# Attention scores on four 64x64 quadrants of TensorE instead of two 64x128 halves, with 192 keys a tile instead of 256

## The chip, the cores and the metric

The kernel runs on one core of one Trainium2 chip. A core has a matrix engine (TensorE, PE in the profile; its weight loads are shown as PEld), a vector engine (VectorE, DVE), a scalar engine (ScalarE, ACT), GpSimd (POOL) and SyncE (SP), which issues the DMAs here. PE reads SBUF and writes PSUM, which has eight banks of 512 fp32 values on each of 128 partitions. The metric is the device time of one execution in microseconds (us), lower is better; the time before is the median of three runs.

## The reference

Eight batches of eight heads, 576 positions, head size 64. Attention is causal in a window of 128 keys, with a linear bias by distance; its result goes through a gated feed-forward layer. Cut to what matters:

```python
scores = scale * np.matmul(q, k.transpose(0, 1, 3, 2))
rel = pos[:, None] - pos[None, :]
bias = slopes[:, None, None] * (-np.abs(rel))[None]
mask = (rel >= 0) & (rel < 128)
scores = np.where(mask, scores + bias[None], -1e9)
attn = softmax(scores)                     # max subtracted
x = np.matmul(attn, v)                     # heads side by side: 4608 tokens x 512
out = (sigmoid(x @ w_gate) * (x @ w_val)) @ w_out      # 512 -> 1536 -> 512
```

Each query sees exactly 128 keys (fewer at the start of a sequence): its own and the 127 before it.

## The kernel before

**Units and blocks.** Two heads of a batch make a unit, 32 units in all. The two sequences of a unit stand one behind the other, 1152 positions, cut in nine blocks of 128 queries. A block needs the keys of its own block and of the block before; block 0 has only its own.

**Scores** (`scores`, L373 to L417). Blocks are taken in groups, of four for the first 72 blocks (18 groups) and of eight after that (27 groups). Head size 64 is the contraction, so a score matmul uses only half the rows of PE: the queries of alternate blocks are laid in partitions 0 to 63 and in 64 to 127 (`by_parity` on the host; keys are stored twice, once in each half), so that two blocks run in the two row halves. For each block one fp32 matmul (L390) has the 128 queries as its stationary operand and 256 keys (block 0: 128) moving. It writes 128 partitions (queries) by 256 columns (keys of the block before, then of its own) of PSUM. A bank holds two such tiles; the banks `mm2` to `mm5` (`sp`) serve the scores, the row halves in different ones. PE records each fp32 matmul as two passes, each with its own weight load.

**Folding.** Of the 256 columns a query needs 128. A predicated copy on DVE (L403) takes, for each pair of tiles in a bank, every column of the own block that lies in the query's future and puts the score of the same column of the block before in its place; `before` is the mask, an upper triangle of ones. Then DVE adds the bias and finds the extreme of each row (L411, biases in `relm`), ACT takes the exponential (L414).

**Probabilities and values.** For three blocks at a time: reciprocal of the sums (DVE, L429, L431), the scaling (ACT L434 or DVE L435), a transpose on PE (L439) into bank `mm6`, a copy to SBUF (`both`, ACT), and two selections on POOL (L450) that spread each column to own and previous keys. For each unit 13 matmuls (L476) multiply with the values; they have 64 stationary columns, so the two heads use the two column halves of PE.

**Feed-forward.** A third of its first projection (L528, banks `mm0` and `mm1`) over the first 3072 tokens is mixed in between the attention steps, once four units of a batch are done. The rest (L662) and the output projection (L780) use a block form with seven products for eight and come after the attention. Their weights are unpacked and split in two parts by ACT and DVE (`prepare`, `prepare2`).

**What sets the order.** Every step is added to a `Graph` with its engine, an estimated cost, what it reads and writes and a wish `want`. `Graph.order` plays a list schedule: of all steps that are ready it takes the one that could start first, and steps of ACT may be moved to DVE or from DVE to POOL. All engines' instructions are then emitted by planned start. A cost thus moves instructions on every engine. While PE has little to do at the very start, `warm` matmuls (L252) fill it.

**At the start** DVE builds the masks and biases (L219 to L236) before the planned steps begin.

The names that the steps below use: L390 score matmul, L403 fold, L411 bias and extreme, L439 transpose, L476 values, L528 first projection.

Of the kernel before, what the change touches and what calls it, by code (L numbers as in the profile page):

```python
# [9 lines left out]
I32 = mybir.dt.int32  # L10
F32R = mybir.dt.float32r
AF = mybir.ActivationFunctionType
ALU = mybir.AluOpType
PSUM = bass.MemoryType.PSUM

P = 128
B, H, S, D = 8, 8, 576, 64
# [137 lines left out]
def dve_cost(n, psum=False, two=False):  # L155
    return 0.07 + n * (0.00104 if psum or two else 0.00053)
# [7 lines left out]
def attention_gated_ffn(ctx: ExitStack, tc: tile.TileContext, qd, kd, vd, wg, wv, wo, out):  # L164
    nc = tc.nc
# [39 lines left out]
    rel = moe.tile([P, 3, P], F32, tag="pi0", name="rel")  # L205
# [4 lines left out]
    def keep(tag, *shape):  # L210
        n, (t, a) = 1, spare.get(tag) or (moe.tile([P, (2 if tag[0] == "h" else KC) * 2 * N2], F32, tag=tag, name=f"early_{tag}"), 0)
        for x in shape:
            n *= x
        spare[tag] = t, a + n
        names = " ".join("abc"[:len(shape)])
        return t[:, a:a + n].rearrange(f"p ({names}) -> p {names}", **dict(zip("abc", shape)))

    before = keep("h3", 2, P).bitcast(I32)
    nc.vector.tensor_scalar(rel[:, 1], rel[:, 0], 0.0, None, op0=ALU.is_lt)  # L219
    for a in range(2):  # L220
        nc.vector.tensor_copy(before[:, a], rel[:, 1])
    nc.vector.scalar_tensor_tensor(rel[:, 2], rel[:, 1], float(P), rel[:, 0], op0=ALU.mult, op1=ALU.add)
    relm = [keep("h3" if p < 2 else "h4", 5, P) for p in range(NPAIR)]
    f = -8.0 * 2.0 ** -1
# [19 lines left out]

    mm = [ps_m.tile([P, NB], F32, name=f"mm{i}") for i in range(8)]
    sp = [t.rearrange("p (a q) -> p a q", a=2) for t in mm[2:6]]
    tp, avp = mm[6].rearrange("p (a q) -> p a q", a=4), mm[7]
    TP, TAIL, AVP = ("mm", 6), ("mm", 6, TRI), ("mm", 7)

# [99 lines left out]
    def slot(x, u, shape):  # L349
        return slots[x] if u.l == NSLOT - 1 and x in slots else T(att, f"{x}{u.l}", [P, *shape], F32)  # L350

    kraw = lambda u: slot("kr", u, [TOK])
    qraw = lambda u: slot("qr", u, [(NBLK + 1) // 2, P])
# [15 lines left out]
    def three_of(u, i):  # L369
        m = u.n * TRI + i // TRI  # L370
        e = i % TRI
        st = lambda: T(att, f"st{m % NST}", [P, 9], F32)
        pb = lambda: T(att, f"pb{m % NPB}", [P, TRI, P], F32) if m % NPB > 1 else kept[m % NPB]  # L373
        return m, e, st, pb, ("st", m % NST), ("pb", m % NPB)

    def scores(blks):

        u0, i0 = blks[0]
        want = u0.when(i0)
        slack = 0.0 if u0.n < HEAD else SLACK  # L380
        spot = [(k % 2, k // 2) for k in range(len(blks))]
        half = len(blks) == RUN // 2 and stages[0] % 2
        stages[0] += 1
        bank_of = lambda r, a: r * (RUN // 4) + a // 2 + half

        def matmuls():
            for (u, i), (r, a) in zip(blks, spot):
                lo = P if i == 0 else 0
                rows = slice(r * D, r * D + D)
                nc.tensor.matmul(sp[bank_of(r, a)][:, a % 2, lo:], qraw(u)[rows, i // 2],  # L390
                                 kraw(u)[rows, (i - 1) * P + lo:(i + 1) * P], start=True, stop=True)

        used = {}
        for (u, i), (r, a) in zip(blks, spot):
            used.setdefault(bank_of(r, a), []).append((u, i, a % 2))
        cost = sum(max(0.216 if i == 0 else 0.432 for (u, i), (r, b) in zip(blks, spot) if b == a) for a in {a for r, a in spot})
        g.add("PE", cost, matmuls, [("qr", u.l, i) for u, i in blks] + [("kr", u.l, j) for u, i in blks for j in (i - 1, i) if j >= 0],
              [("mm", 2 + b) for b in used], want, slack=slack, release=max(u.rel(i) for u, i in blks), mode=1)
        for b, on in sorted(used.items(), key=lambda kv: blks.index(kv[1][0][:2])):
            a = [a for u, i, a in on if i]  # L400
            if a:
                a0, a1 = a[0], a[-1] + 1
                g.add("DVE", dve_cost((a1 - a0) * P, psum=True), lambda b=b, a0=a0, a1=a1: nc.vector.copy_predicated(  # L403
                    sp[b][:, a0:a1, P:], before[:, a0:a1], sp[b][:, a0:a1, 0:P]), ["before"], [("mm", 2 + b)], want)
        for (u, i), (r, a) in zip(blks, spot):
            def one(u, i, b, a):
                m, e, st, pb, kst, kpb = three_of(u, i)
                want = u.when(i)
                mid = NBLK // 2
                w = 0 if i == 0 else 1 if i < mid else min(4, i - mid + 2)  # L410
                g.add("DVE", 0.21, lambda: nc.vector.tensor_tensor_reduce(  # L411
                    pb()[:, e], sp[b][:, a, P:], relm[u.p][:, w], op0=ALU.add, op1=ALU.min,
                    scale=-0.125, scalar=3.0e38, accum_out=st()[:, e:e + 1]), [("mm", 2 + b)], [(kpb, e), (kst, e)], want)
                g.add("ACT", 0.39, lambda: nc.scalar.activation(  # L414
                    pb()[:, e], pb()[:, e], AF.Exp, bias=st()[:, e:e + 1], scale=-1.0, accum_out=st()[:, 3 + e:4 + e]),
                    [(kst, e)], [(kpb, e), (kst, 3 + e)], want)
            one(u, i, bank_of(r, a), a % 2)  # L417
            if i % TRI == TRI - 1:
                probabilities(u, i - TRI + 1)
            if i == NBLK - 1:  # L420
                values(u)

    def probabilities(u, i0):
        m, _, st, pb, kst, kpb = three_of(u, i0)
        want = u.when(i0 + TRI)
        slack = 0.0 if u.n < HEAD else SLACK
        n, kb = TRI, ("both", m % NBOTH)
        both = lambda: T(att, f"both{m % NBOTH}", [P, TRI, P], F32)
        g.add("DVE", 0.07, lambda: nc.vector.tensor_scalar_add(st()[:, 6:9], st()[:, 3:6], 1.0e-9),  # L429
              [(kst, 3 + e) for e in range(n)], [(kst, 6)], want)  # L430
        g.add("DVE", 0.09, lambda: nc.vector.reciprocal(st()[:, 6:9], st()[:, 6:9]), [], [(kst, 6)], want)  # L431
        for e in range(n):
            args = lambda e=e: (pb()[:, e], pb()[:, e], st()[:, 6 + e:7 + e])
            g.add("ACT", 0.3, lambda args=args: nc.scalar.mul(*args()), [(kst, 6)], [(kpb, e)], want,  # L434
                  ways=[("DVE", 0.16, True, lambda args=args: nc.vector.tensor_scalar_mul(*args()))])  # L435

        def transpose():
            for e in range(n):
                nc.tensor.transpose(tp[:, e], pb()[:, e], ident)  # L439

        g.add("PE", 0.11 * n + 0.1, transpose, [(kpb, e) for e in range(n)], [TP], want, slack=slack)
        copy(lambda: both(), lambda: tp[:, 0:n], n * P, [TP], [kb], want, psum=True)
        for own in range(2):
            step, cmp, mult = ([1, P], ALU.is_ge, -1) if own else ([-1, P], ALU.is_gt, 1)

            def spread(own=own, step=step, cmp=cmp, mult=mult):
                f0 = 2 * i0 + own
                nc.gpsimd.affine_select(pt(u)[:, f0:f0 + 2 * n - 1:2, :], both(), [[0, n], step], cmp, 0.0,  # L450
                                        base=0, channel_multiplier=mult)

            g.add("POOL", 0.13 + 0.12 * n, spread, [kb], [("pt", u.n % NPT, i0 + e, own) for e in range(n)], want)
# [361 lines left out]
    for u in units:  # L815
        if u.n + NSLOT - 1 < len(units):
            load(units[u.n + NSLOT - 1])
        while at < (u.n + 1) * NBLK:
            n = RUN // 2 if at < SOON * NBLK else RUN
            scores(stream[at:at + n])  # L820
            at += n
        if u.n == 0:
            todo = [(src, kind, i) for i0 in range(0, FC1, GRP) for src, kind in ((wg, "g"), (wv, "v")) for i in range(i0, i0 + GRP)]
            for k, (src, kind, i) in enumerate(todo):
                prepare(w1, src, kind, i, W0 + WSTEP * k)
        if u.p == NPAIR - 1:
            while todo1 and (todo1[0] + 1) * NB <= (u.b + 1) * S:
                if todo1[0] >= LATE and banks[0] == 2:
                    banks[0] = 8
                    g.add("PY", 0.0, lambda: None, [], [TP, TAIL], FIRST)  # L830
                ffn(todo1.pop(0), w1)
# [54 lines left out]
    for e in range(4):  # L886
        m, p = 6 + e // 2, e % 2
# [60 lines left out]
```

## Time and profile before

| | |
|---|---|
| median of three runs | 1014.79 us (1013.95 to 1015.31) |
| the profiled execution, its own time | 1015.13 us |
| its span, first to last instruction | 1013.4 us |
| granted TensorE clock | 0.999 |
| PE, PEld, DVE, ACT, POOL busy | 997.5, 927.8, 784.1, 544.6, 125.1 us |
| score matmuls L390, first to last start | 5.1 to 285.8 us |
| values matmuls L476, first to last start | 19.3 to 307.9 us |

Busy time of PE is not PE at its peak: a matmul's record reaches to the end of its pipeline, so records overlap. A row of the grouped view reads: line, engine, operation, tiles written and read, shape, count; then the busy time in us, the mean of one in ns; then the idle time of the engine just before and who ended it. A row of the timeline reads: start in us, length in us, engine, line, operation, tiles, shape of most, count. A row of the chain reads: start, length, what.

### The profile page before, as it was taken

The page shows a single profiled execution, that of the slowest core. Times are in us where ns is not written, and L with a number is a line of the kernel's source. Part 1 is how long each engine was busy: PE and PEld are TensorE (multiplying, and loading weights), DVE is VectorE, ACT ScalarE, POOL GpSimd, SP SyncE. Part 2 cuts the span into 40 slices and gives each one's busy share as a digit, 9 for nine tenths or more (in the row PEclk, how much of TensorE's full clock was granted, in tenths as well). Part 3 has the DMA queues.
Part 4 walks back from the last instruction along what each step waited for, and adds up shares of the span by engine and source line. Part 5 has one row for each costly group of instructions (what it writes and reads, how often), then busy time and mean ns, then how long its engine had stood idle before and what let it go on. Part 6 is the DMA issues. An engine that isn't in the chain of part 4 may idle for free.

```text
span 1013.4 us, 18087 instructions
## 1 busy us (share of the span) xinstructions
PE 997.5 (98%) x6216; PEld 927.8 (92%) x6216; DVE 784.1 (77%) x2025; ACT 544.6 (54%) x1435; POOL 125.1 (12%) x218
## 2 busy tenths in 40 slices
PE   9899899999999999999999999999999999999998
PEld 7677678777888999999999999999999999999998
DVE  7999799967856997964976768848478877869783
ACT  6899879768753545533553535435354443434341
POOL 2343344323330000000000000000000000000000
PEclk9999999999999999999999999999999999999999
DMA  8777677847434452411553453536886354543501
GB/s 287 252 253 260 218 243 233 289 153 230 156 123 157 146 177 85 141 63 63 200 190 120 144 184 121 197 138 219 325 332 196 102 168 139 161 149 102 179 24 63
DMA packets 84284, 176.82 MB, mean 174 GB/s; under 512 B 7648, under 2 KB 50016, under 8 KB 84192
## 3 DMA queue, kind: packets, MB, share of 16 engines
q1 hardware_dynamic: 84192, 175.67, 51.2%
q8 instruction: 49, 0.80, 0.3%
q14 instruction: 43, 0.35, 0.1%
HBM read 117.44 MB, written 58.20 MB: 173 GB/s over the span
## 4 chain that ended last, share of the span: by engine, by line
PE 83%; DVE 8%; ACT 5%; DMA 2%; issue 1%; SPq 0%; ACTq 0%; DVEq 0%
PE mm L662 38%; PE mm L780 26%; PE mm L528 8%; PE mm L476 4%; PE mm L390 4%; PE mm L439 2%; ACT pb L414 2%; ACT both L185 1%; DVE first L194 1%; ACT pb L434 1%; DVE mm L403 1%; DMA wraw<-in_moe_w_gate_dram 1%; DVE w2s L194 1%; DVE pb L411 1%; DMA early_xr<-xs 1%
## 5 line engine op out<-in xcount | busy, mean ns | idle before, releaser
L662 PE MATMUL mm<-xc,w2s 128*128 128x384 f32 x2352 | 410.2, 335 | 1.0 <-ACT low L185 0.9
L662 PEld LDWEIGHTS mm<-xc,w2s 128*128 128x128 f32 x2352 | 407.4, 188 | 3.8 <-ACT low L185 2.2
L780 PE MATMUL mm<-duo,wo 128*128 128x384 f32 x1512 | 262.2, 334 | 0.0
L780 PEld LDWEIGHTS mm<-duo,wo 128*128 128x128 f32 x1512 | 262.1, 188 | 0.0
L528 PE MATMUL mm<-first,first 128*128 128x512 f32 x564 | 148.6, 403 | 0.7 <-DVE early_hs L547 0.4
L450 POOL TENSOR_SCALAR_AFFINE_SELECT pt<-both 128x384 f32<-128x384 f32 x192 | 106.6, 579 | 191.7 <-ACT both L185 178.3
L528 PEld LDWEIGHTS mm<-first,first 128*128 128x128 f32 x564 | 100.6, 188 | 21.3 <-issue 1.3
L673 ACT ACTIVATE sg<-mm 128x384 f32<-128x384 f32 x112 | 54.9, 492 | 115.9 <-PE mm L662 63.6
L669 DVE TENSOR_TENSOR mm<-mm,low 128x384 f32<-128x384 f32 x112 | 63.0, 564 | 70.0 <-PE mm L662 66.4
L185 ACT COPY low<-mm 128x384 f32<-128x384 f32 x110 | 53.0, 481 | 75.9 <-PE mm L662 64.6
L414 ACT ACTIVATE pb<-pb,st 128x128 f32<-128x128 f32 x216 | 85.0, 400 | 8.9 <-DVE st L411 8.8
L476 PEld LDWEIGHTS mm<-pt,vr 128*64 128x64 f32 x832 | 61.2, 137 | 12.7 <-issue 7.6
L194 DVE TENSOR_TENSOR duo<-rows,duo 128x768 fp32r<-128x768 f32 x66 | 62.9, 957 | 10.6 <-ACT duo L185 8.6
L185 ACT CAST duo<-rows 128x768 fp32r<-128x768 f32 x48 | 40.0, 837 | 54.1 <-PE mm L780 29.5
L476 PE MATMUL mm<-pt,vr 128*64 128x256 f32 (+2 forms) x832 | 67.4, 306 | 0.6 <-POOL pt L450 0.6
L185 ACT COPY both<-mm 128x384 f32<-128x384 f32 x96 | 46.0, 479 | 34.6 <-PE mm L439 23.5
L403 DVE COPY_PREDICATED mm<-early_h,mm 128x256 f32<-128x256 int32 (+1 forms) x144 | 49.2, 392 | 9.8 <-PE mm L390 9.3
L390 PE MATMUL mm<-kr,qr 64*128 64x256 f32 (+1 forms) x396 | 55.1, 381 | 0.2 <-DMA kr<-in_k_dram 0.2
L411 DVE CUSTOM_DVE_ANT_0 pb<-mm,early_h 128x128 f32<-128x128 f32 x216 | 51.7, 282 | 0.0
L390 PEld LDWEIGHTS mm<-kr,qr 64*128 64x128 f32 x396 | 38.1, 186 | 9.4 <-issue 2.3
L439 PE MATMUL mm<-ident,pb 128*128 128x128 f32 x216 | 38.1, 284 | 7.1 <-ACT both L185 5.9
L439 PEld LDWEIGHTS mm<-ident,pb 128*128 128x128 f32 x216 | 24.7, 140 | 21.3 <-ACT both L185 9.8
(117 smaller groups left out, 1128.0 us busy)
## 6 DMA issues: line engine op xcount, KB each, us to landing
hid<-later_hs SPq DMA_DIRECT2D x56, 384.0 KB, 2.3
rows<-hid SPq DMA_DIRECT2D x48, 384.0 KB, 3.9
kr<-in_k_dram SPq DMA_DIRECT2D x21, 576.0 KB, 4.4
wo<-stash_o SPq DMA_DIRECT2D x12, 896.0 KB, 7.7
vr<-in_v_dram SPq DMA_DIRECT2D x32, 288.0 KB, 3.2
xs<-xt SPq DMA_DIRECT2D x32, 288.0 KB, 2.8
stash_o<-wtmp SPq DMA_DIRECT2D x12, 768.0 KB, 3.4
rows_xr<-hid SPq DMA_DIRECT2D x24, 384.0 KB, 3.4
```

The costliest lines, as they stand in the source:

```text
L185: g.add("ACT", act_cost(n, psum), lambda: nc.scalar.copy(out(), src()), reads, writes, want, release=release, ways=[("DVE", dve_cost(n, ps ...
L194: g.add("DVE", dve_cost(n, psum, True), lambda: nc.vector.tensor_tensor(out(), a(), b(), op=ALU.subtract), reads, writes, want, port=not p ...
L390: nc.tensor.matmul(sp[bank_of(r, a)][:, a % 2, lo:], qraw(u)[rows, i // 2], kraw(u)[rows, (i - 1) * P + lo:(i + 1) * P], start=True, stop= ...
L411: g.add("DVE", 0.21, lambda: nc.vector.tensor_tensor_reduce(pb()[:, e], sp[b][:, a, P:], relm[u.p][:, w], op0=ALU.add, op1=ALU.min, scale= ...
L414: g.add("ACT", 0.39, lambda: nc.scalar.activation(pb()[:, e], pb()[:, e], AF.Exp, bias=st()[:, e:e + 1], scale=-1.0, accum_out=st()[:, 3 + ...
L439: nc.tensor.transpose(tp[:, e], pb()[:, e], ident)
L450: nc.gpsimd.affine_select(pt(u)[:, f0:f0 + 2 * n - 1:2, :], both(), [[0, n], step], cmp, 0.0, base=0, channel_multiplier=mult)
L476: nc.tensor.matmul(to()[e * D:(e + 1) * D, a - e * S - t0:b - e * S - t0], vraw(u)[:, c], seen, start=first, stop=last, skip_group_check=True)
L528: nc.tensor.matmul(mm[s][:, 0:wd], w.tile(kind, wi, i)[:, c * P:(c + 1) * P], xpart(x, c)[:, 0:wd], start=(k == 0 and c == 0), stop=(k == ...
L662: nc.tensor.matmul(mm[b][:, 0:N2], w.tile2(i, wp)[:, wk, c * P:(c + 1) * P], combo(k, xp)[:, c], start=(start and c == 0 and j == 0), stop ...
L669: g.add("DVE", dve_cost(N2, psum=True), lambda: nc.vector.tensor_tensor(o(), bk(b)(), a(), op=ALU.add), [("mm", b), *reads] if okeys else ...
L780: nc.tensor.matmul(mm[b][:, 0:N2], wo2(2 * q + m, wp)[:, k, j * P:(j + 1) * P], duo(xp)[:, m], start=(k in (0, 3, 1) and q == 0 and m == 0 ...
```

## The change

Each block of 128 queries becomes two tiles of 64 queries. The stationary operand has 64 rows (head size) and 64 columns (queries), so a tile uses one quadrant of PE: the row half is that of the block as before, and the first 64 queries write PSUM partitions 0 to 63, the last 64 write 64 to 127. A 64-query tile needs three runs of 64 keys, 192 instead of 256. A block's PSUM tile keeps its 256 columns, seen as four slots of 64, and slots 1 and 2 are where the folded scores end:

- first 64 queries: slots 1, 2, 3 get the keys in reversed order of runs, own first half, previous second half, previous first half; slot 0 is not written by a matmul
- last 64 queries: slots 0, 1, 2 get previous second half, own first half, own second half; slot 3 is not written

One predicated copy per pair of tiles, as before, takes slot 3 into slot 1 and slot 0 into slot 2 where the mask says so; the mask is now zero for the first 64 queries in slot 2. The slots that no matmul writes are set to zero once at the start, since the copy reads them. Block 0 of a sequence writes slots 1 and 2 only. The planner's cost of a pair of full blocks goes from 0.432 to 0.33; nothing else of it is changed.

```diff
-    before = keep("h3", 2, P).bitcast(I32)
+    before = keep("h3", 4, D).bitcast(I32).rearrange("p (a s) q -> p a s q", a=2)
     nc.vector.tensor_scalar(rel[:, 1], rel[:, 0], 0.0, None, op0=ALU.is_lt)
     for a in range(2):
-        nc.vector.tensor_copy(before[:, a], rel[:, 1])
+        nc.vector.tensor_copy(before[:, a], rel[:, 1].rearrange("p (s q) -> p s q", q=D))
+        nc.vector.memset(before[0:D, a, 1], 0)
...
     sp = [t.rearrange("p (a q) -> p a q", a=2) for t in mm[2:6]]
+    for t in sp:
+        nc.vector.memset(t.rearrange("p a (s q) -> p a s q", q=D)[:, :, 0::3], 0.0)
...
+        quads = lambda b: sp[b].rearrange("p a (s q) -> p a s q", q=D)
         def matmuls():
+            todo = [[] for _ in range((len(blks) + 1) // 2)]
+            order = [a for a in range(len(todo)) for h in range(2)]
             for (u, i), (r, a) in zip(blks, spot):
-                lo = P if i == 0 else 0
-                rows = slice(r * D, r * D + D)
-                nc.tensor.matmul(sp[bank_of(r, a)][:, a % 2, lo:], qraw(u)[rows, i // 2],
-                                 kraw(u)[rows, (i - 1) * P + lo:(i + 1) * P], start=True, stop=True)
+                todo[a].append((u, i, r, a))
+            for h in (0, 1) * len(todo):
+                for u, i, r, a in todo[order.pop(0)]:
+                    rows = slice(r * D, r * D + D)
+                    keys = kraw(u)[rows].rearrange("p (t q) -> p t q", q=D)
+                    to = quads(bank_of(r, a))[h * D:(h + 1) * D, a % 2]
+                    if i == 0:
+                        to, keys = to[:, 1:3], keys[:, 0:2]
+                    elif h == 0:
+                        last = 2 * i - 3
+                        to, keys = to[:, 1:4], keys[:, 2 * i:(last if last >= 0 else None):-1]
+                    else:
+                        to, keys = to[:, 0:3], keys[:, 2 * i - 1:2 * i + 2]
+                    nc.tensor.matmul(to, qraw(u)[rows, i // 2, h * D:(h + 1) * D], keys, start=True, stop=True)
...
-        cost = sum(max(0.216 if i == 0 else 0.432 for (u, i), (r, b) in zip(blks, spot) if b == a) for a in {a for r, a in spot})
+        cost = sum(max(0.216 if i == 0 else 0.33 for (u, i), (r, b) in zip(blks, spot) if b == a) for a in {a for r, a in spot})
...
-                    sp[b][:, a0:a1, P:], before[:, a0:a1], sp[b][:, a0:a1, 0:P]), ["before"], [("mm", 2 + b)], want)
+                    quads(b)[:, a0:a1, 1:3], before[:, a0:a1], quads(b)[:, a0:a1, 3::-3]), ["before"], [("mm", 2 + b)], want)
...
-                    pb()[:, e], sp[b][:, a, P:], relm[u.p][:, w], op0=ALU.add, op1=ALU.min,
+                    pb()[:, e], sp[b][:, a, D:D + P], relm[u.p][:, w], op0=ALU.add, op1=ALU.min,
```

On PE, a group of eight blocks in the middle of the attention reads before as follows (`mm2` to `mm5` are the score banks, `kr1` and `early_h2` keys, `qr1` and `early_xr` queries; the shape is partitions by columns written):

```order
L390 MATMUL mm2_148<-kr1_172,qr1_174 128x256
L390 MATMUL mm4_150<-early_h2_154,early_xr_155 128x128
L390 MATMUL mm2_148<-early_h2_154,early_xr_155 128x256
L390 MATMUL mm4_150<-early_h2_154,early_xr_155 128x256
L390 MATMUL mm3_149<-early_h2_154,early_xr_155 128x256
L390 MATMUL mm5_151<-early_h2_154,early_xr_155 128x256
```

The two rows that follow repeat the last two. Now such a group (another one, near the same place) ends as follows; the eight rows ahead of these are the same with `mm2` and `mm4`, and the score line is now L408:

```order
L408 MATMUL mm3_151<-kr1_178,qr1_180 64x192
L408 MATMUL mm5_153<-kr1_178,qr1_180 64x192
L408 MATMUL mm3_151<-kr1_178,qr1_180 64x192
L408 MATMUL mm5_153<-kr1_178,qr1_180 64x192
L408 MATMUL mm3_151<-early_h2_160,early_xr_161 64x128
L408 MATMUL mm5_153<-early_h2_160,early_xr_161 64x192
L408 MATMUL mm3_151<-early_h2_160,early_xr_161 64x128
L408 MATMUL mm5_153<-early_h2_160,early_xr_161 64x192
```

Eight matmuls became sixteen; of a pair of blocks the two first halves stand ahead of the two second halves, row halves alternating.

On DVE, the end of the preparation and the first folds read before (`early_h3` holds masks and the first biases, `early_h4` biases):

```order
L236 TENSOR_SCALAR early_h3_78<-early_h3_78 128x640
L236 TENSOR_SCALAR early_h4_83<-early_h3_78 128x640 x2
L403 COPY_PREDICATED mm2_148<-early_h3_78,mm2_148 128x128
L403 COPY_PREDICATED mm4_150<-early_h3_78,mm4_150 128x2x128
L411 ISA early_h2_154,st0_194<-mm2_148,early_h3_78 128x128
```

and now:

```order
L237 TENSOR_SCALAR early_h3_78<-early_h3_78 128x640
L237 TENSOR_SCALAR early_h4_85<-early_h3_78 128x640 x2
L249 MEMSET mm2_150 128x2x2x64
L249 MEMSET mm3_151 128x2x2x64
L249 MEMSET mm4_152 128x2x2x64
L249 MEMSET mm5_153 128x2x2x64
L420 COPY_PREDICATED mm2_150<-early_h3_78,mm2_150 128x128
L420 COPY_PREDICATED mm4_152<-early_h3_78,mm4_152 128x2x128
```

Four writes to PSUM have come between the biases and the first fold; the folds themselves keep their place and shape.

## The prediction

> **What bounds the kernel now.** I read the page first, for the span and the share of each engine, then the windows, to see where the engines are full, then the chain of work that ended last.
>
> ```profile
> span 1013.4 us, 18087 instructions
> PE 997.5 (98%) x6216; PEld 927.8 (92%) x6216; DVE 784.1 (77%) x2025; ACT 544.6 (54%) x1435; POOL 125.1 (12%) x218
> PE 83%; DVE 8%; ACT 5%; DMA 2%; issue 1%; SPq 0%; ACTq 0%; DVEq 0%
> ```
>
> TensorE holds 83% of the chain. The change lies in the attention stage alone, so the mean over the span is not enough. The windows (columns: PE, weight loads, DVE, ACT, POOL, each busy time and count) cut that stage in three:
>
> ```profile
> 20.00:130.00 110.00, 100.66 (x797) 77.14 (x794) 98.32 (x469) 98.97 (x381) 41.62 (x72) 1.00 0.73 247
> 130.00:180.00 50.00, 49.59 (x368) 39.42 (x366) 45.67 (x195) 44.73 (x161) 24.06 (x38) 1.00 0.75 237
> 180.00:290.00 110.00, 109.90 (x804) 87.94 (x806) 86.62 (x461) 81.20 (x315) 33.99 (x67) 1.00 0.61 201
> ```
>
> Up to 130 us PE leaves 9.3 of 110 us idle, and DVE and ACT leave 11.7 and 11.0: three engines, closely coupled. From 130 on PE has no idle time, while DVE and ACT still have a tenth to a quarter. The chain says the same. At 85 us it runs over ACT; from 186 us it runs over PE, score matmuls (L390) included. At 85 us:
>
> ```profile
> 85.41 0.58 ACT pb L414 x3
> 85.98 0.58 ACT xt L185 x2
> 86.56 0.28 ACT both L185
> 86.83 0.75 ACT pb L414 x3
> ```
>
> and from 186 us:
>
> ```profile
> 193.69 0.33 PE mm L439 x3
> 194.02 1.93 PE mm L390 x15
> 195.95 2.01 PE mm L476 x24
> 197.96 0.48 PE mm L439 x3
> 198.43 1.63 PE mm L528 x7
> ```
>
> So a shorter score step is worth its full length from about 182 us, little before 130 us.
>
> **The change, part by part.** *One score group.* The timeline has a group of eight blocks (16 records, since each matmul is recorded as two passes, each with its own weight load) and a group of four. The four:
>
> ```profile
> 25.82 1.13 PE L390 MATMUL mm<-kr,qr 64*128 64x256 f32 x8
> ```
>
> and the eight:
>
> ```profile
> 105.03 1.99 PE L390 MATMUL mm<-kr,qr 64*128 64x256 f32 x16
> ```
>
> Four blocks more cost 0.86 us. They are four passes more on each half of the rows (two blocks of two passes), and the halves run side by side, so a pass of 256 keys takes 0.86/4 = 0.215 us, and 1.99 - 8 x 0.215 = 0.27 us is fixed. With 192 keys a pass takes 0.215 x 192/256 = 0.161 us, if four quadrants run as fully side by side as two halves do now. The fixed part holds one weight load that nothing covers. Its size goes by columns:
>
> ```profile
> L390 PEld LDWEIGHTS mm<-kr,qr 64*128 64x128 f32 x396 | 38.1, 186 | 9.4 <-issue 2.3 <-DVE st L431 1.1 <-DVE st L411 0.9
> L476 PEld LDWEIGHTS mm<-pt,vr 128*64 128x64 f32 x832 | 61.2, 137 | 12.7 <-issue 7.6 <-POOL pt L450 4.0
> ```
>
> 64 columns instead of 128 save 186 - 137 = 49 ns. A group of eight then takes 8 x 0.161 + 0.22 = 1.51 us, 0.48 less; a group of four saves 4 x 0.054 + 0.05 = 0.265. The first block of a sequence has 128 keys before and after; it stands in one half only, and the other half's chain of full blocks sets the length, so it changes nothing.
>
> *Do four run at once?* No row shows 64 x 64 tiles. Two row halves run at once (L390), and two column halves over all rows do (L476). What matters is whether a tile waits for matmuls ahead of it in the program that belong to another tile. Its program order in each set of values matmuls is:
>
> ```order
> L476 MATMUL mm_153<-pt_469,vr_184 64x256
> L476 MATMUL mm_153<-pt_469,vr_184 64x192
> L476 MATMUL mm_153<-pt_469,vr_184 64x256 x4
> L476 MATMUL mm_153<-pt_469,vr_184 64x128
> L476 MATMUL mm_153<-pt_469,vr_184 64x192
> ```
>
> The last two are head 0 (first columns, 128 wide) and then head 1 (other columns, 192 wide). Two stretches of 10 ns of one such set, 40 ns apart, grouped by form, show what is in flight. The first, at 108.74 us:
>
> ```profile
> L476 PE MATMUL mm<-pt,vr 128*64 128x256 f32 x2 | 0.5, 379 | 0.0
> L476 PE MATMUL mm<-pt,vr 128*64 128x192 f32 x1 | 0.3, 326 | 0.0
> ```
>
> and the second, at 108.78 us:
>
> ```profile
> L476 PE MATMUL mm<-pt,vr 128*64 128x256 f32 x2 | 0.5, 379 | 0.0
> L476 PE MATMUL mm<-pt,vr 128*64 128x192 f32 x1 | 0.3, 326 | 0.0
> L476 PE MATMUL mm<-pt,vr 128*64 128x128 f32 x1 | 0.3, 272 | 0.0
> ```
>
> The 192-wide one has started while the 128-wide one, which stands ahead of it, has not; that one joins only later. So a column tile overtakes both passes of the other tile's matmul. [...]
>
> The weight loads have to keep up too. At the end of a set, matmuls of 64 columns follow each other:
>
> ```profile
> L476 PE MATMUL mm<-pt,vr 128*64 128x64 f32 x8 | 0.4, 221 | 0.0
> ```
>
> Eight are in flight in one 10 ns stretch, 221 ns each: one starts every 28 ns, and each has its own load of 64 columns. Four quadrants need four in 161 ns, and 4 x 28 = 112. I therefore take 0.161.
>
> *Where the groups stand.* Counts of the line's records in 131 to 182 us:
>
> ```profile
> L390 PE MATMUL mm<-kr,qr x70: 269/376/480, 131.9 to 175.5; 64*128 64x256 f32 x64, 64*128 64x128 f32 x6
> L390 PE MATMUL mm<-early_h,early_xr x26: 269/376/480, 147.9 to 176.3; 64*128 64x256 f32 x22, 64*128 64x128 f32 x4
> ```
>
> and in 182 to 300 us:
>
> ```profile
> L390 PE MATMUL mm<-kr,qr x144: 269/376/480, 187.7 to 285.8; 64*128 64x256 f32 x128, 64*128 64x128 f32 x16
> L390 PE MATMUL mm<-early_h,early_xr x64: 269/376/480, 186.7 to 268.7; 64*128 64x256 f32 x58, 64*128 64x128 f32 x6
> ```
>
> 208/16 = 13 groups after 182 us: 13 x 0.48 = 6.2 us, all on the path. 96/16 = 6 groups before that, 2.9 us; there DVE and ACT have only about 10% left, so I take half, 1.4. The program has 18 groups of four and 27 of eight, so 18 of four and 8 of eight lie earlier: 18 x 0.265 + 8 x 0.48 = 8.6 us, of which between none and all reaches the end. PE had 8% idle there and its work is not what is late, so I take a sixth, 1.4.
>
> *The start.* The new writes of zero stand on DVE ahead of the first fold. What stands there now, first DVE's preparation:
>
> ```profile
> 3.59 0.11 DVE L231 MEMSET early_h<- 64x64 f32 x1
> ```
>
> then its last step and the first fold:
>
> ```profile
> 4.33 1.30 DVE L236 TENSOR_SCALAR early_h<-early_h 128x640 f32<-128x640 f32 x3
> 6.07 0.29 DVE L403 COPY_PREDICATED mm<-early_h,mm 128x128 f32<-128x128 int32 x1 [0.45 <-PE mm L390]
> ```
>
> and PE's first score matmuls:
>
> ```profile
> 5.12 0.92 PE L390 MATMUL mm<-kr,qr 64*128 64x128 f32 x6
> 6.24 1.66 PE L390 MATMUL mm<-kr,qr 64*128 64x256 f32 x10 [0.21 <-DMA kr<-in_k_dram]
> ```
>
> Two writes of 64 elements add 2 x 0.11. The four to PSUM have 256 elements each, and no row shows such a write. Below stands a write of 64, 0.11 us; above, a fold of 256, 0.42 us (next rows). The slope of the folds, 1.05 ns an element, makes it 0.11 + 192 x 0.00105 = 0.31, nearest to the upper end; 1.2 us for four. DVE is then free for the first fold at 5.63 + 1.5 = 7.1 us, and since PE must wait for the zeros in the third bank (about 6.8 us instead of 5.12), the first fold comes at about 7.6 instead of 6.07. Until now the second part of the keys (6.24 us) came later than that need, so some of the delay is swallowed: between 0.8 and 1.5 us, I take 1.3. Behind these writes on DVE stand all folds, exponent offsets and so ACT, and nothing there hides it.
>
> *The fold* writes as many elements as before, but its source has a step of -192 between runs of 64.
>
> ```profile
> L403 DVE COPY_PREDICATED mm<-early_h,mm 128x256 f32<-128x256 int32 x112 | 43.4, 422 | 8.7 <-PE mm L390 8.2
> L403 DVE COPY_PREDICATED mm<-early_h,mm 128x128 f32<-128x128 int32 x32 | 9.2, 287 | 1.1 <-PE mm L390 1.1
> ```
>
> The 256-element form already jumps once between its two tiles and costs (422 - 287)/128 = 1.05 ns an element, no more than one element a DVE step, so a jump is free here: zero. The ends are zero and what two separate folds would cost, 2 x 287 - 422 = 152 ns each (a gain is excluded, since no element goes). *The order* of the later stages, as built, stands as before after the last values set, up to some nine matmuls of 576 of the first projection that move ahead of it: zero.
>
> The sum, against this execution's own 1015.13 us (span 1013.4): 1015.1 - 6.2 - 1.4 - 1.4 + 1.3 = 1007.4. This execution is 0.34 us above the median of the three runs, 1014.79, so I forecast **1007.0**.
>
> **The rivals.** *Two abreast (slower).* If PE lets only two quadrants run at once, a pair of blocks needs 8 quadrant passes in four steps of 0.161 in place of two of 0.215. A group of eight takes 16 x 0.161 + 0.22 = 2.80, 0.81 more; 19 groups are 15.4 us, the earlier ones (8 x 0.81 + 18 x 0.38 = 13.3) would first fill the 9.3 us that PE has idle, so perhaps 4 more; with the start, 1015 + 15 + 4 + 1 = 1035. It decides from 0.43/0.161 = 2.7 quadrants abreast downwards. For it: a fourth quadrant must overtake three matmuls and the trace shows one overtaken. Against it: a tile that is one step late stays one step late, so overtaking one is enough for four abreast in the long run. Chance 0.13.
>
> *The loads bind.* If four loads of 64 columns came one after the other at their 49 ns, a pass would take 0.196 in place of 0.161, a group 1.79, 0.20 less than now: 13 x 0.20 + half of 6 x 0.20 - 1.3, 1012 to 1014. The eight in flight speak against it. [...] Chance 0.06.
>
> *DVE and ACT take over.* If every microsecond freed on PE before 182 us turns into waiting, and DVE's 87 of 110 us later come in bursts, or the planner's new order opens a hole of a few microseconds, half of the 6.2 remains: 1015 - 3.1 + 1.3 = 1013. Chance 0.14. *The fold gets slower* by the 152 ns: 58 folds in 20 to 130 us, where DVE is full, make 8.8 us and eat the gain, 1016. Chance 0.05.
>
> **How the numbers follow.** My forecast has 0.62; its own range goes from all groups on the path (18 x 0.265 + 27 x 0.48 = 17.7, less 1.3, 998.4) to a loss of a third of it, 1010. The range to 1016 takes in the loads, DVE and ACT, and the fold, and leaves out the two abreast (0.13) and some 0.04 below 999. A measurement of this kernel tells about 0.2%, 2 us, from no change: faster is the forecast, and most of the third rival and half of the loads, 0.73; the same is the rest of those and the fold, 0.12; slower the two abreast and bad draws of order, 0.15.
>
> **What would show it.** Right: groups of 32 records in about 1.5 us, 64x192 matmuls starting four close together; last values set some 8 us earlier; fold means of 422 and 287; first fold near 7.5 us. Wrong: groups at 1.8 us (loads) or 2.8 (two abreast); PE idle time before L439 growing by as much as L390 shrinks (DVE and ACT); a fold near 570.

## The result and the profile after

| | before | after |
|---|---|---|
| median, same chip | 1014.64 us (5 runs, 1013.95 to 1015.31) | 1008.75 us (5 runs, 1008.59 to 1010.94) |
| ratio of the times | | 0.9948 (95%: 0.9933 to 0.9962) |
| profiled execution, span | 1013.4 us | 1007.0 us |
| granted TensorE clock | 0.999 | 0.995; 0.993 in the run of 1009.59 us, 0.990 in that of 1010.94 us |

By the medians the kernel is 5.9 us faster; the forecast was 1007.0, and its terms added up to 7.7 us. The page of after, with the clock that was granted in 40 slices of the span:

```profile
span 1007.0 us, 19232 instructions
PE 985.4 (98%) x6790; PEld 920.5 (91%) x6790; DVE 781.0 (78%) x2039; ACT 540.4 (54%) x1428; POOL 121.9 (12%) x217
...
PEclk9899999999999999999999999999999999999999
...
PE 89%; ACT 5%; DVE 5%; issue 1%; POOL 0%; ACTq 0%; POOLq 0%
```

PE has 574 records more (288 score matmuls more, of two passes each, and one filler matmul less) and 12 us less busy time. The second slice, 25 to 50 us, is new: the clock was not full there.

The matmuls themselves do what the forecast said. A group of eight in the timeline of after, and what PE has in flight in 10 ns shortly after its start:

```profile
253.50 1.53 PE L408 MATMUL mm<-kr,qr 64*64 64x192 f32 x32
```

```profile
L408 PE MATMUL mm<-kr,qr 64*64 64x192 f32 x4 | 0.4, 374 | 0.0
```

1.53 us in place of 1.99, forecast 1.51, with matmuls of four quadrants in flight in that stretch. The folds and the new writes of zero, in the grouped view of after:

```profile
L420 DVE COPY_PREDICATED mm<-early_h,mm 128x256 f32<-128x256 int32 x112 | 42.9, 422 | 8.3 <-PE mm L408 8.1
...
L420 DVE COPY_PREDICATED mm<-early_h,mm 128x128 f32<-128x128 int32 x32 | 9.2, 289 | 2.2 <-PE mm L408 2.1
...
L249 DVE MEMSET mm<- 128x256 f32 x4 | 1.1, 272 | 0.1
```

The source with a step of -192 costs the fold nothing (422 and 289 ns, were 422 and 287). A write of zero took 272 ns, estimated 310. The stage windows of after, to be read against those of before:

```profile
20.00:130.00 110.00, 96.29 (x1004) 74.07 (x995) 97.01 (x474) 95.04 (x368) 43.29 (x74) 0.95 0.72 243
130.00:180.00 50.00, 49.27 (x490) 39.61 (x489) 45.59 (x206) 42.28 (x161) 23.45 (x40) 1.00 0.77 248
180.00:290.00 110.00, 110.00 (x1057) 88.45 (x1056) 88.50 (x465) 87.99 (x335) 37.35 (x73) 1.00 0.64 205
```

From 20 to 130 us PE, DVE and ACT are all less busy than before: the stretch holds more idle time on all three, and the mean clock there is 0.95. From 180 us PE is full, as before.

### The profile page after: what moved, and what is told of

Its sections match the earlier page's. It is cut to its first block, busy times and chain, and to the rows that moved or that the text cites. A ratio compares the mean times of both kernels' runs of the same rounds, so it can differ in the third digit from the quotient of the medians.

```text
span 1007.0 us, 19232 instructions
## 1 busy us (share of the span) xinstructions
PE 985.4 (98%) x6790; PEld 920.5 (91%) x6790; DVE 781.0 (78%) x2039; ACT 540.4 (54%) x1428; POOL 121.9 (12%) x217
## 4 chain that ended last, share of the span: by engine, by line
PE 89%; ACT 5%; DVE 5%; issue 1%; POOL 0%; ACTq 0%; POOLq 0%
PE mm L679 40%; PE mm L797 26%; PE mm L545 10%; PE mm L493 5%; PE mm L408 4%; PE mm L456 3%; ACT pb L431 2%; ACT both L185 1%; ACT pb L451 1%; PE mm L255 1%; DVE xc L194 0%; DVE early_hs L564 0%; DVE w2s L194 0%; DVE mm L420 0%; DVE first L194 0%
## 5 line engine op out<-in xcount | busy, mean ns | idle before, releaser
L545 PE MATMUL mm<-first,first 128*128 128x512 f32 x564 | 154.1, 409 | 1.6 <-DVE first L194 1.5
L467 POOL TENSOR_SCALAR_AFFINE_SELECT pt<-both 128x384 f32<-128x384 f32 x192 | 103.8, 564 | 188.5 <-ACT both L185 165.1
L194 DVE TENSOR_TENSOR duo<-rows,duo 128x768 fp32r<-128x768 f32 x66 | 62.9, 956 | 9.8 <-ACT duo L185 7.9
L185 ACT CAST duo<-rows 128x768 fp32r<-128x768 f32 x44 | 36.7, 835 | 48.7 <-PE mm L797 26.0
L420 DVE COPY_PREDICATED mm<-early_h,mm 128x256 f32<-128x256 int32 (+1 forms) x144 | 48.5, 392 | 10.5 <-PE mm L408 10.2
L456 PE MATMUL mm<-ident,pb 128*128 128x128 f32 x216 | 38.3, 286 | 10.9 <-ACT both L185 8.9
L408 PE MATMUL mm<-kr,qr 64*64 64x192 f32 (+1 forms) x792 | 44.8, 337 | 1.4 <-DVE mm L249 1.1
L431 ACT ACTIVATION_READ_ACCUMULATOR pb<-pb,st 128x1 f32 x216 | 42.7, 198 | 0.0
```

The costliest lines, as they stand in the source:

```text
L185: g.add("ACT", act_cost(n, psum), lambda: nc.scalar.copy(out(), src()), reads, writes, want, release=release, ways=[("DVE", dve_cost(n, ps ...
L194: g.add("DVE", dve_cost(n, psum, True), lambda: nc.vector.tensor_tensor(out(), a(), b(), op=ALU.subtract), reads, writes, want, port=not p ...
L408: nc.tensor.matmul(to, qraw(u)[rows, i // 2, h * D:(h + 1) * D], keys, start=True, stop=True)
L431: g.add("ACT", 0.39, lambda: nc.scalar.activation(pb()[:, e], pb()[:, e], AF.Exp, bias=st()[:, e:e + 1], scale=-1.0, accum_out=st()[:, 3 + ...
L545: nc.tensor.matmul(mm[s][:, 0:wd], w.tile(kind, wi, i)[:, c * P:(c + 1) * P], xpart(x, c)[:, 0:wd], start=(k == 0 and c == 0), stop=(k == ...
```

## The experiments

Each was timed beside the kernel before on its own chip (medians of before 1014.1 to 1014.7 us), so ratios are compared. Two theories stood for the 1.8 us that were missing: **clock** (TensorE, with less to do, is so idle in the stretch that DVE and ACT bound that its clock falls) and **order** (the planner, told a lower cost, lays the steps worse). The start was a third question, and the reach of TensorE past waiting matmuls a fourth.

**e1, filler matmuls for longer.**

```diff
-WARM = 30.0
+WARM = 46.4
```

> The changed kernel, with the filler matmuls on TensorE kept up until the first projection needs their bank (planned time 46 instead of 30 us). Theory 'clock': the faster scores leave TensorE so idle in the first 50 us that its clock falls to half (6.8 us at 44 us and 3.4 us at 119 us in the profile after); the first dip goes, granted clock 0.998 or more, and 1.2 to 2 us are won: 1007.0 to 1007.5. Rival 'hidden': DVE and ACT bound that stretch, so a slow TensorE costs nothing there: clock up, time 1008.7 as after. Rival 'order': the loss comes from the new order of steps, which the filler does not change: 1008.7.

Measured: 1006.20 us, ratio 0.9920 (0.9906 to 0.9933), clock 0.999. Three windows from 40 us, after first:

```profile
40.00:44.00 4.00, 2.11 (x22) 1.32 (x22) 4.00 (x27) 4.00 (x20) 0.99 (x2) 1.00 0.88 270
44.00:48.00 4.00, 1.48 (x9) 0.79 (x13) 3.96 (x22) 4.00 (x19) 0.99 (x2) 0.54 0.57 213
48.00:52.00 4.00, 4.00 (x40) 2.98 (x34) 3.94 (x18) 3.06 (x10) 1.23 (x3) 0.61 0.57 178
```

and e1:

```profile
40.00:44.00 4.00, 3.66 (x40) 3.34 (x41) 4.00 (x31) 4.00 (x19) 1.87 (x4) 1.00 0.96 369
44.00:48.00 4.00, 3.53 (x49) 2.87 (x48) 3.97 (x14) 4.00 (x16) 0.75 (x2) 1.00 0.27 64
48.00:52.00 4.00, 4.00 (x37) 3.32 (x37) 4.00 (x20) 3.96 (x16) 1.99 (x4) 1.00 0.65 223
```

In after PE is busy for 2.11 of 4 us; then the clock (last column but two) falls to half, by the clock's record from 44.3 us on and for 6.8 us, while DVE and ACT are full. With filler it stays up (1.00 in the three windows of e1). A second drop in after, 3.4 us at 119 us, is gone too (1.00 in e1 from 116 to 124 us), though no filler stands there; it also followed a window in which PE had little to do:

```profile
116.00:120.00 4.00, 1.74 (x6) 1.10 (x7) 4.00 (x24) 3.17 (x14) 1.14 (x3) 0.92 1.00 363
120.00:124.00 4.00, 4.00 (x13) 3.11 (x13) 3.96 (x12) 3.18 (x13) 1.29 (x2) 0.65 0.27 100
```

The steps are in the same order, so 0.28 points of the ratio, 2.8 us, go with the filler. 'Hidden' falls. The four runs of e1 stood at 1005.4 and 1007.0, twice each. The profile is of a run of 1005.35, and what it shows of the start (under e3) means that not all of the 2.8 us is the drops.

**e2, the old cost for the planner, new matmuls.**

```diff
-        cost = sum(max(0.216 if i == 0 else 0.33 for (u, i), (r, b) in zip(blks, spot) if b == a) for a in {a for r, a in spot})
+        cost = sum(max(0.216 if i == 0 else 0.432 for (u, i), (r, b) in zip(blks, spot) if b == a) for a in {a for r, a in spot})
```

> The changed kernel, with the planner's old cost of a score group (0.432 in place of 0.33), so that the steps stand in the order of before while the matmuls are the new ones. Theory 'order': the holes in the first 130 us come from the new order; clock 0.998 or more and about 1006.8. Theory 'clock': TensorE does less work in that stretch in any order, the dips stay in some place, 1008 to 1010, clock 0.993 to 0.996.

Measured: 1007.88 us, 0.9939 (0.9926 to 0.9951), clock 1.000 in the profile. But one of the five runs had 0.998, and so had three of the five of e10, which has the same order. So the clock fell in some runs of this order too, only less than 'clock' held; and the time is not the 1006.8 of 'order' either. It can't be told from that of after. This run is the best place to see where the gain is made, since all steps stand as before. Four sets of values matmuls in the timeline of before, from three windows:

```profile
117.08 1.29 PE L476 MATMUL mm<-pt,vr 128*64 128x256 f32 x10
```

```profile
181.79 1.51 PE L476 MATMUL mm<-pt,vr 128*64 128x256 f32 x12
```

```profile
306.02 1.29 PE L476 MATMUL mm<-pt,vr 128*64 128x256 f32 x10
```

and the same sets in e2:

```profile
116.99 1.29 PE L493 MATMUL mm<-pt,vr 128*64 128x256 f32 x10
```

```profile
180.69 2.08 PE L493 MATMUL mm<-pt,vr 128*64 128x256 f32 x26
```

```profile
299.62 1.62 PE L493 MATMUL mm<-pt,vr 128*64 128x256 f32 x14
```

Up to 117 us 0.09 us are won, by 182 us 1.10, by the last set 6.40. So in these two executions the groups in the first 117 us are worth nothing, and those after 182 us 5.3 us.

**e3, the writes of zero at the head of DVE's program.** DVE waits for POOL there until 1.6 us.

```diff
+    mm = [ps_m.tile([P, NB], F32, name=f"mm{i}") for i in range(8)]
+    sp = [t.rearrange("p (a q) -> p a q", a=2) for t in mm[2:6]]
+    for t in sp:
+        nc.vector.memset(t.rearrange("p a (s q) -> p a s q", q=D)[:, :, 0::3], 0.0)
     ident = const.tile([P, P], F32, name="ident")
...
-    mm = [ps_m.tile([P, NB], F32, name=f"mm{i}") for i in range(8)]
-    sp = [t.rearrange("p (a q) -> p a q", a=2) for t in mm[2:6]]
-    for t in sp:
-        nc.vector.memset(t.rearrange("p a (s q) -> p a s q", q=D)[:, :, 0::3], 0.0)
```

> The changed kernel, with the four writes of zero to PSUM moved to the head of DVE's program, where it waits for POOL until 1.6 us. If the start is on the path as forecast, about 1.0 us less than after: 1007.7. If what follows swallows it: 1008.7.

Measured: 1006.87 us, 0.9931 (0.9919 to 0.9943), clock 0.995: 0.17 points less than after, 1.7 us and not 1.0, though the two intervals overlap. The first scores and folds of after:

```profile
6.26 3.38 PE L408 MATMUL mm<-kr,qr 64*64 64x128 f32 x32 [1.06 <-DVE mm L249]
...
8.40 0.63 DVE L420 COPY_PREDICATED mm<-early_h,mm 128x128 f32<-128x128 int32 x2 [1.37 <-PE mm L408]
```

of e1, which has the writes at the same place:

```profile
6.26 2.07 PE L408 MATMUL mm<-kr,qr 64*64 64x128 f32 x32 [1.05 <-DVE mm L249]
...
7.72 0.63 DVE L420 COPY_PREDICATED mm<-early_h,mm 128x128 f32<-128x128 int32 x2 [0.70 <-PE mm L408]
```

and the fold of e3:

```profile
6.82 0.63 DVE L420 COPY_PREDICATED mm<-early_h,mm 128x128 f32<-128x128 int32 x2 [0.62 <-PE mm L408]
```

The same 32 records that start at the same time take 3.38 us in after and 2.07 in e1: in after PE had not yet come to full clock (the clock's record has it full from 10.2 us on; from 5.0 in before, where no such wait stands). e6, with the writes in the same place, has half clock until 10.7 us; but e1, with a wait for the zeros of 1.05 us against 1.06, has the short records. Whether the wait or chance puts the rise off was not tested by itself. The first and the last start of the values matmuls, of after:

```profile
L493 PE MATMUL mm<-pt,vr x832: 218/326/431, 20.9 to 304.2; 128*64 128x256 f32 x65, 128*64 128x64 f32 x64, 128*64 128x192 f32 x25, 128*64 128x128 f32 x13
```

of e1:

```profile
L493 PE MATMUL mm<-pt,vr x832: 219/326/431, 19.4 to 300.9; 128*64 128x256 f32 x65, 128*64 128x64 f32 x64, 128*64 128x192 f32 x25, 128*64 128x128 f32 x13
```

and of e3:

```profile
L493 PE MATMUL mm<-pt,vr x832: 219/326/431, 18.6 to 302.1; 128*64 128x256 f32 x65, 128*64 128x64 f32 x64, 128*64 128x192 f32 x25, 128*64 128x128 f32 x13
```

At the first values e1 is 0.8 us behind e3, about the length of the wait, and after 1.5 us behind e1, with the late rise. e1's two values are 1.6 us apart, which would fit, but no run of 1007.0 has a profile. From the first values to the last, after takes 283.3 us, e3, with the same mean clock of 0.995, 283.5, and e1, with 0.999, 281.5. So the two drops cost about 1.9 us, an estimate.

**e4, the old matmuls with the new cost.** The kernel before, and nothing else than:

```diff
-        cost = sum(max(0.216 if i == 0 else 0.432 for (u, i), (r, b) in zip(blks, spot) if b == a) for a in {a for r, a in spot})
+        cost = sum(max(0.216 if i == 0 else 0.33 for (u, i), (r, b) in zip(blks, spot) if b == a) for a in {a for r, a in spot})
```

> The kernel before, with only the planner's cost of a score group changed to the new 0.33. Theory 'order': the new order alone costs 2 us or more, 1016.5 to 1018. Theory 'clock': the old matmuls keep TensorE busy, clock 0.999, within 1 us of before, 1013.6 to 1015.6.

Measured: 1019.75 us, 1.0050 (1.0037 to 1.0064), clock 0.997. The order alone makes the old kernel 5 us slower, more than either theory had, and in this order the clock drops with the old matmuls too: its mean from 20 to 130 us is 0.97, where before has 1.00. Of 110 us that takes at most about 3.3 us of TensorE's work, so it is not all of the 5. The two theories are therefore hard to part: in that stretch the order leaves PE without work for longer (98.70 us busy, 100.66 in before), and the clock falls too. With the new matmuls the order costs far less: after and e2, which differ in it alone, are 0.09 points apart, inside both intervals.

**e5, all second halves last**, and **e11, two pairs at a time.** Only the order inside a group changes. In e5:

```diff
-            order = [a for a in range(len(todo)) for h in range(2)]
+            order = list(range(len(todo))) * 2
...
-            for h in (0, 1) * len(todo):
+            for h in [0] * len(todo) + [1] * len(todo):
```

and in e11:

```diff
-            order = [a for a in range(len(todo)) for h in range(2)]
+            order = [a for b in range(0, len(todo), 2) for h in range(2) for a in range(b, b + 2)]
...
-            for h in (0, 1) * len(todo):
+            for h in (0, 0, 1, 1) * (len(todo) // 2):
```

> The changed kernel, with the order inside a score group changed: the first halves of all blocks of the group, then the second halves, so that four quadrants run at once only if a second half overtakes all first halves still to come (up to 14 passes on TensorE). If TensorE lets a quadrant overtake any number: groups of eight stay at 1.53 us, time 1008 to 1010. If it overtakes only a few, as the rival 'two abreast' held: groups of eight grow towards 16 x 0.161 + 0.2 = 2.8 us, and the time by 10 to 25 us.

> The changed kernel, with the first halves of two pairs of blocks, then their second halves. In the run with all second halves last, the first second half started when six passes of first halves were still ahead of it. Here seven at the most are to be overtaken (two row halves, two blocks, two passes, less the one that runs). If six is the reach, groups of eight take 1.53 to 1.70 us and the time stays within 1008 to 1012; if the reach is a number of instructions that also counts weight loads done, groups of 1.7 to 1.9 us and 1012 to 1016.

Measured: e5 1024.07 us (before 1014.12) and e11 1009.38 us (before 1014.36), one run each. A group of eight in e5:

```profile
138.36 2.23 PE L408 MATMUL mm<-kr,qr 64*64 64x192 f32 x32
```

and in e11:

```profile
253.92 1.58 PE L408 MATMUL mm<-kr,qr 64*64 64x192 f32 x32
```

e5 loses 2.23 - 1.53 = 0.70 us, 4.3 steps of 0.161: of the sixteen passes of first halves six were still ahead when the first second half started. In e11 six are ahead from the outset (eight passes, two running), and only 0.05 us is lost. So six passes were overtaken in e5, and with sixteen ahead at the outset 0.70 us were lost; where between the two orders the loss begins was not tested. In the order as shipped four passes of first halves stand ahead of a pair's second halves, and the group takes 1.53 us.

**e6, quadrants in the groups of eight only.** Groups of four keep the row halves, 256 keys, the old mask and the old cost:

```diff
...
+        old = len(blks) == RUN // 2
         def matmuls():
+            if old:
+                for (u, i), (r, a) in zip(blks, spot):
+                    lo = P if i == 0 else 0
+                    rows = slice(r * D, r * D + D)
+                    nc.tensor.matmul(sp[bank_of(r, a)][:, a % 2, lo:], qraw(u)[rows, i // 2],
+                                     kraw(u)[rows, (i - 1) * P + lo:(i + 1) * P], start=True, stop=True)
+                return
...
-        cost = sum(max(0.216 if i == 0 else 0.33 for (u, i), (r, b) in zip(blks, spot) if b == a) for a in {a for r, a in spot})
+        cost = sum(max(0.216 if i == 0 else 0.432 if old else 0.33 for (u, i), (r, b) in zip(blks, spot) if b == a) for a in {a for r, a in spot})
...
```

> The changed kernel, with the first 18 score groups (of four blocks) in the old form: two row halves, 256 keys, old mask and old planner cost; quadrants only in the 27 groups of eight. Theory 'clock': TensorE stays busier in the first 45 us, the dip at 44 us goes, clock 0.997 or more, and the time is 1007 to 1008 although 18 x 0.27 = 4.8 us of TensorE work come back. If early groups are worth their length after all: 1010 to 1013.

Measured: 1005.89 us, 0.9919 (0.9906 to 0.9933), clock 0.998. Faster than after with 4.8 us more work for PE (18 x 0.265, an estimate; a group of four takes 1.13 us in the old form and 0.87 in the new), and 1 us under what 'clock' expected. In place of after's drops, 10.2 us in all, one of 3.4 us stands at 55 us. Part of the gain is order: see e12.

**e7 to e9, put together.** e7 is the edits of e1 and e3 together; e8 those of e6 and e3; e9 is e8 with

```diff
-WARM = 30.0
+WARM = 42.5
```

> The filler matmuls kept up to 46 us and the writes of zero moved to the head of DVE's program, together. If both terms are real and add up: 1006.0 to 1006.7. If neither is: 1008.7.

> Quadrants only in the groups of eight, and the writes of zero at the head of DVE's program. The profile of the run with quadrants in eights alone shows the clock at half until 10.7 us and for 3.4 us at 55 us. If the writes of zero delay the clock's rise, it now rises by 5.5 us and the time falls by 1 to 2 us: 1004.0 to 1005.0. If the start is swallowed: 1005.9.

> As the run before it, and the filler matmuls kept up to 42.5 us of planned time. If the dip at 55 us costs anything, 0.5 to 1 us less than the run before it and clock 0.999; if not, the same.

Measured: e7 1006.71 us, 0.9920 (0.9906 to 0.9933); e8 1003.43 us, 0.9894 (0.9879 to 0.9909); e9 1002.77 us, 0.9886 (0.9873 to 0.9900). e7 misses: no better than e1, with a clock of 0.997 to 0.998 in its five runs (e1 0.999 in three of four), so the terms do not add. Why the clock fell there was not tested. In e8 the terms add, and the time is a little below the expected range; e9 is below it by less than the intervals can tell. In e9 every run has a clock of 0.999 or 1.000, in e8 only the profiled one has 0.998.

**e10, old cost and early zeros.** The edits of e2 and e3 together.

> Old planner cost (order of before), quadrants everywhere, writes of zero at the head. With the old order alone the profile had the same start as before (first values at 19.2 us) and no dip. Theory: nothing to win at the start in that order, 1007.3 to 1008.0. Rival: the 1.1 us of the writes are on the path there too, 1006.5 to 1007.0.

Measured: 1007.30 us, 0.9932 (0.9919 to 0.9945), against 0.9939 of e2: no difference that can be told. But three of e10's five runs, the profiled one among them, have a clock of 0.998, so a gain at the start may be hidden behind it. That the start is covered in the order of before is not shown.

**e12, the order of e9 with quadrants everywhere.** The kernel of e3 with `WARM = 42.5` and

```diff
-        cost = sum(max(0.216 if i == 0 else 0.33 for (u, i), (r, b) in zip(blks, spot) if b == a) for a in {a for r, a in spot})
+        cost = sum(max(0.216 if i == 0 else 0.432 if len(blks) == RUN // 2 else 0.33 for (u, i), (r, b) in zip(blks, spot) if b == a) for a in {a for r, a in spot})
```

It differs from e9 only in the matmuls, masks and folds of the first 18 groups.

> The kernel of e9 (writes of zero at the head, filler up to 42.5 us, planner cost 0.432 in groups of four and 0.33 in groups of eight, so the same order of steps), but with quadrants in the first 18 groups too: only the form of their matmuls differs from e9. If the early groups were worth their length: 18 x 0.265 = 4.8 us less than e9, 998. If nothing of TensorE's work there is on the path: within 0.7 us of e9's 1002.8. If the lighter work lets the clock fall in spite of the filler: 1004 or more with a clock under 0.998.

Measured: 1002.47 us, 0.9880 (0.9862 to 0.9898), against 0.9886 of e9. 4.8 us (by the estimate above) of TensorE's work less in the first 18 groups change nothing that can be measured, although the mean clock of the profile from 20 to 130 us is 0.98, and 1.00 in that of e9. With e9 this is the best version: 1.2% under before and about 0.7% under the kernel as changed. Its early window:

```profile
20.00:130.00 110.00, 100.05 (x1052) 77.81 (x1051) 101.45 (x487) 99.94 (x381) 45.42 (x74) 0.98 0.74 249
```

DVE is now busy for 101.45 of 110 us in place of 97.01, PE for 100.05 in place of 96.29: more work is done in this stretch. What PE has left of the first projection behind the last values set shows which. In e12:

```profile
L545 PE MATMUL mm<-first,first x83: 389/389/501, 303.9 to 322.8; 128*128 128x512 f32 x83
```

and in e7, whose matmuls are the same:

```profile
L545 PE MATMUL mm<-first,first x115: 388/390/502, 302.1 to 328.5; 128*128 128x512 f32 x115
```

With the one and the two that stand in a row of their own these are 84 passes and 117. The last values set of e12 starts 1.8 us later than that of e7, but its first projection ends 5.7 us earlier. The old cost of the first 18 groups makes a plan that puts 33 passes more ahead of the last values set, where PE had idle time. e6, e8 and e9 have 84 there as well, after, e1 and e3 117, before and e2 126.

## Why the prediction was right, and which terms were off

- *One score group*: forecast 0.48 us less, measured 0.46 (1.99 to 1.53). Four quadrants run at once (four 64x192 records in flight at 253.60 us in after), the loads keep up (1.53 us; the estimate for loads in a row was 1.79), and block 0, which that group holds, does not lengthen it. Right.
- *Do four run at once*: the two stretches of the values matmuls told it. In e5 too, second halves start ahead of passes that stand before them in the program, six in the group's record. The argument that overtaking one is enough was not needed; it was not tested by itself.
- *After 182 us*: forecast 6.2, 5.3 in the order of before (e2). *131 to 182 us*: forecast 1.4; 1.0 between 117 and 182 us. Both right, a little large.
- *Before 131 us*: forecast 1.4, measured 0.1 (e2, up to 117 us) and nothing (e12 against e9). This term was wrong: shorter matmuls only made PE's idle time there longer. From 20 to 130 us it grew from 9.3 to 15.1 us in e2 (94.95 us busy, were 100.66).
- *The start*: forecast 1.3, measured 1.7 (e3); by the first values, 0.8 for the wait (e1 against e3) and 1.5 more where the clock rises late (after). The delay of the first fold was forecast to 7.6 us and came to 7.72 where the clock was up (e1) and 8.40 where it was not (after).
- *The fold* and *what comes after the attention*: zero was right for the fold (422 and 289 ns, were 422 and 287). Its slope of 1.05 ns an element is also that of additions on DVE in before without a jump (L194: 957 ns for 768 elements, 1754 for 1536, so 1.04). Behind the attention, nine passes of the first projection fewer stand after the last values set (117, were 126), as forecast. e2's span is 7.6 us below before's and its last values set 6.4, so 1.2 us come later; by the medians e2 is only 6.5 us below, so about as much is chance of the two executions.
- What the sum left out was the clock, 1.9 us for the two drops. The sign and the range stand, but the planner's cost was treated as a matter of order alone ("up to some nine matmuls"), and only behind the attention; e4 shows 5 us of it, clock included, with the old matmuls, and e12 against e7 some 4 us with the new ones, in the part ahead. That part of the rival 'DVE and ACT take over' which spoke of the planner's new order opening a hole came true, beside the forecast and not in its place: PE's idle time before the transposes grew from 7.1 to 10.9 us.
- *The last values set* was to come some 8 us earlier. It came 3.6 us earlier in after (304.2, was 307.9), with nine more passes of the first projection ahead of it, and 7.0 in e1. So the total owes something to luck: the terms ahead of the last values set were too large by 2.6 us together (e2), and what was lost on clock and start seems in part made up by the order, which the sum had at nothing. In e1, with the new order, more filler and a clock of 0.999 in its profile, the gain is 8.2 us by the medians; in e2, with the old order, 6.5.

In the clock's record of after, the first four stretches between one change and the next, from its rise on, are 34.13, 6.83, 68.27 and 3.41 us: 10, 2, 20 and 1 times 3.413. Counted from the rise in steps of that length, three windows in which PE had little to do:

```profile
23.82:27.23 3.41, 1.63 (x15) 1.44 (x14) 3.26 (x19) 3.41 (x16) 1.63 (x4) 1.00 0.42 139
40.89:44.30 3.41, 1.56 (x19) 1.00 (x19) 3.41 (x23) 3.41 (x16) 0.99 (x2) 1.00 0.92 287
115.98:119.39 3.41, 1.25 (x5) 0.61 (x5) 3.41 (x19) 2.58 (x10) 1.16 (x3) 1.00 1.02 376
```

The first kept the clock, the other two were followed by half clock. PE was busy for 2.63 us or more in every other window of after that was at full clock, up to 990 us, and those kept it. In before, counted in the same way, the least is 2.21 us (from 49.41 us), and the clock stays full up to 1012.0 us. PE was idle for a whole one in neither. What decides a fall these two profiles do not show. The runs of after get longer as their clock gets lower (0.995: 1008.59 to 1008.75; 0.993: 1009.59; 0.990: 1010.94); why it differs between runs was not tested.

What stays open: how much of the loss in the first 130 us is order and how much is clock. e12 against e7 is 0.4 points, 4 us, with the cost of the first 18 groups (and 4 us of filler time) as the difference. The clock differs between their profiles as well (0.998 and 0.997), but at the same mean clock of 0.998 e7 took 1005.34 and 1005.51 us and e12 1002.56 and 1002.99, so some 3 of the 4 us are not the clock. For after no such pair is on record.

## What to carry to other kernels

Here small matmuls in quadrants were worth nearly their full saving only where TensorE ends last (in e2 5.3 us of 6.2 after 182 us, 0.09 us up to 117); cut the trace by stage before multiplying a saving by a count. Where a list scheduler plans with costs, a truer cost for one engine can make a worse plan in a stretch that other engines bound (e7 against e12): measure the new cost with the old instructions, and the old cost with the new ones. And where work is taken from TensorE in a stretch in which it waits, look at the granted clock afterwards; in e1 filler matmuls there kept it up (1.00 from 40 to 52 us, 0.54 and 0.61 in after), and in e9 they cost nothing that could be measured (1002.77 us, 1003.43 without). They are no guarantee: in the profile of e12, with the filler of e9, it was 0.98 from 20 to 130 us.

## What the hardware did that was not expected

- In e5 matmuls of a free quadrant started ahead of six passes that stood before them, and a group of eight took 2.23 us; in e11, with six ahead from the outset, it took 1.58, in after 1.53.
- In after the clock went to half after windows of 3.41 us in which TensorE was busy, not idle: for 1.56 and 1.25 us, while after one with 1.63 us it stayed full.
- The rise to full clock came at 10.2 us in after, where a wait of 1.06 us stood in the first microseconds, and the first 32 passes of scores took 3.38 us; in e1, with a wait of 1.05 us there, they took 2.07.
